# A second place for transposed exponentials, a planner that counts transfers at a shared rate, and ten pairs with native scores

## The chip, the core and the metric

One core of a Trainium2 chip runs the whole computation. The metric is the device time of one execution in microseconds. Five engines work side by side, each on its own instruction stream in program order: TensorE (PE in the profile, with its weight loads as PEld), VectorE (DVE), ScalarE (ACT), GpSimd (POOL) and SyncE (SP). Here SyncE does nothing but start DMA transfers, one after the other, and it too waits at the head of its queue.

## What is computed

The reference computes attention with a block-causal mask (blocks of 64) for 8 batches of 8 heads, 576 positions, head size 64, and then a bilinear feed-forward of its result (4608 tokens, width 512, inner width 1536).

```python
scores = scale * np.matmul(q, k.transpose(0, 1, 3, 2))
scores = np.where(block_i >= block_j, scores, -1000000000.0)
attn = np.exp(scores - np.max(scores, axis=-1, keepdims=True))
attn = attn / (np.sum(attn, axis=-1, keepdims=True) + 1e-09)
x = np.matmul(attn, v)            # heads side by side
out = (x @ w_a) * (x @ w_b) @ w_out
```

The feed-forward weights come as 64-bit floats, read as pairs of 32-bit words: the kernel itself converts them to two 32-bit parts ("hi" and "lo").

## The kernel before

The work falls in two. First comes attention, two heads at a time ("pair" p, 32 of them, four to a batch), with a first feed-forward pass over the first third of the inner width (`F1 = 4` blocks of 128) woven between. Then come two more passes over the rest of the width (from line 1077 on), which TensorE fills alone. Names carry batch and head: `x1_6` belongs to batch 1, heads 6 and 7, which is pair 7.

Most products are made from "split" operands: a value is a high part plus a low part, and three products (hi hi, hi lo, lo hi) make one. Scores of the first `NATIVE` pairs are instead made by one plain 32-bit product that the program writes as one matmul and the profile shows as two; such a pair needs a scaling of q on GpSimd (L448). Other pairs need four steps: `qh` and `kh` on ScalarE (L454, L462), `ql` on VectorE (L458), `kl` on GpSimd (L466).

A pair goes through these steps:

- SyncE loads q and k (`take`, L397) and v (L402).
- TensorE makes scores in two rounds, because there are only two score banks in PSUM, `x` and `y`: first `C3` and `C1`, then, when the exponentials have freed the banks, `C2` and `C0` (L482).
- VectorE masks and takes negated maxima (L501, L509 to L518); ScalarE makes exponentials with their sums (L528); VectorE adds and inverts the sums (`rc`, L557 to L562); GpSimd normalizes in ten steps (L571).
- The exponentials have to be transposed. For pairs 0 to 3 TensorE does it and ScalarE copies the result into the tile `at` (L593, L599). From pair 4 on VectorE transposes blocks of 32 by 32 into a tile `bl` (L576, L581; there are two, for even and odd pairs), and SyncE starts 16 copies per pair that carry the blocks to their partitions in `at` (`move`, L621). There is one `at`: a pair's copies wait for the value product of the pair before.
- TensorE makes the value product (60 matmuls, L630). ScalarE evacuates it into `xf` (L648, L649), SyncE stores it (L663), and ScalarE and GpSimd split it (L669, L673).

The first pass of the feed-forward, once a batch's four pairs are through, consists of groups of 12 matmuls (L234): per half batch eight groups for the two inner products, whose product is split again (`hf` on VectorE L722, `hh` on ScalarE, `hl` on GpSimd), and four groups for the output (`pso`). They have the lowest priority on TensorE and run strictly in order; this text calls them fillers.

At the start twelve weight conversions (steps `cd`, `cs`, `cr`, `cm`, `cf`, `cg`, `cx`, `ch`, `cl`, L863 to L876) run beside the first pairs, six of the steps on VectorE and ScalarE between the attention's. They use a raw tile with two buffers (`fetch`, L136) and three scratch tiles `s`, `m`, `x`. A second lot of conversions for the later passes starts after the last pair's scores (`start_conv2`).

The order of everything up to the last pair is set by a planner (`plan`, L342). It holds a table `TOOK` (engine time, time until others see the result) for each kind of step, plays the steps through, and always takes the ready step with the lowest key on the engine that is free first; the result is written down engine by engine, and the chip follows that order. `SLOTS` gives the keys of a pair's steps relative to others, `CONV_STEP` the keys and earliest times of the conversions. It is a plan only: on the chip an instruction starts when the real semaphores allow it.

```python
last_v = [got("V", p - 1)]
...
ds = ... [Op("D", SP_, lambda i=i, g=g: move(i, g), [o for o in (got("T", p), got("V", p - 1)) if o], ...
```

Of the kernel before, what the change touches and what calls it, by code (L numbers as in the profile page):

```python
# [9 lines left out]
F32 = mybir.dt.float32  # L10
F32R = mybir.dt.float32r
I32 = mybir.dt.int32
# [8 lines left out]
EPS = 1e-9  # L21
WARM = 9

NATIVE = 6
MM = 3
MORE = 8 - MM
XB = 3
PET = 4
A_KEY = 18
SLOTS = [12.0] * 6 + [14.6] * 26  # L30
CONV_STEP = 6.5
CONV_KEY = 12.0
CONV_LO = True
KEEP_UNTIL, KEEP_EVERY = 66.0, 2.5
SWITCH = 0.1
LAGS = {"PE": 0.24, "DVE": 0.14, "Activation": 0.17, "Pool": 0.1, "SP": 2.0}
TOOK = {
# [12 lines left out]
    "posta": (0.29, 0.17, 0), "postb": (0.375, 0.14, 0), "posto": (0.29, 0.17, 0), "hh": (0.338, 0.16, 0),  # L50
# [16 lines left out]
def attention_then_bilinear_ffn(  # L67
# [65 lines left out]
            tc.add_manual_dep(ins.ins, last[key].ins.name, NOSYNC, reason="after work that is waited for")  # L133


    def fetch(src, nm):  # L136
        raw = wpool.tile([P, 512, 2], I32, tag="raw", name=f"raw{nm}", bufs=2)
        nc.sync.dma_start(raw.rearrange("p n w -> p (n w)"), src)
        return raw

    def convert(raw, nm, paced, own=False):

        hi, mid = raw[:, :, 1], raw.bitcast(U16)[:, :, 1]
        s, m, x = (wpool.tile([P, 512], I32, tag=f"cv_{x}", name=f"{x}{nm}") for x in "smx")
        sf, mf, xf = (t.bitcast(F32) for t in (s, m, x))
        v = nc.vector

        def step(ins):
            if paced:
                behind_of(ins, "hf")  # L150


        step(v.tensor_scalar(s, hi, 20, 0x7FF, op0=ALU.logical_shift_right, op1=ALU.bitwise_and))
        nc.scalar.activation(s, s, AF.Relu, scale=2.0 ** 23, bias=shift)
        yield

        step(v.tensor_scalar(m, hi, 0xFFFFF, 0x100000, op0=ALU.bitwise_and, op1=ALU.bitwise_or))
        yield
        step(v.scalar_tensor_tensor(mf, mid, 2.0 ** -16, m, op0=ALU.mult, op1=ALU.add))
        yield  # L160
        step(v.scalar_tensor_tensor(s, hi, -0x80000000, s, op0=ALU.bitwise_and, op1=ALU.bitwise_or))
        yield
        step(v.tensor_tensor(xf, mf, sf, op=ALU.mult))
        if own:
            yield
        return xf, mf
# [71 lines left out]
    hpool = pool(ctx, "hpool", 1)  # L238

    def h_tile(kind, n, dt, nm):  # L240
        return hpool.tile([P, T2], dt, tag=f"h{kind}", name=nm, bufs=(10, 6)[kind])[:, :n]

    def ab_unit(f, xs, n, nm, hs):

# [97 lines left out]
    def plan():  # L342
        free = dict.fromkeys(LAGS, 0.0)
        ready = {e: [] for e in LAGS}
        users = [[] for _ in ops]
        left = [len(o.deps) for o in ops]
        for o in ops:
            for d, plus in o.deps:
                users[d.n].append((o, plus))
            if not o.deps:  # L350
                ready[o.eng].append(o)
        out = []
        mode = 0
        held = []

        def since(o):
            if not o.frees:
                return o.at
            if len(held) < MM:
                return o.at  # L360
            r = held[-MM]
            return o.at if r is o else 1e9 if r.end is None else max(o.at, r.end)

        while any(ready.values()):
            t, e = min((max(free[e], min(map(since, q))), e) for e, q in ready.items() if q)
            o = min((o for o in ready[e] if since(o) <= t), key=lambda o: (o.key, o.n))
            if o.frees:
                held.append(o.frees)
            ready[e].remove(o)
            free[e] = t + o.took + (SWITCH if e == PE_ and o.mode != mode else 0)  # L370
            if e == PE_:
                mode = o.mode
            if o.also:
                free[ACT_] = max(free[ACT_], t) + o.also
            o.start, o.end = t, free[e] + o.lag
            out.append(o)
            for u, plus in users[o.n]:
                u.at = max(u.at, o.end + plus)
                left[u.n] -= 1
                if not left[u.n]:  # L380
                    ready[u.eng].append(u)
        assert len(out) == len(ops)
        return out
# [37 lines left out]
    def got(what, p):  # L421
        return done.get((what, p))

    def attention(p):
# [158 lines left out]

        def new_at():
            if "at" not in st:
                st["at"] = apool.tile([P, NQ, 2, NE_, QB], F32, tag="at", name=f"at{n}", bufs=1)
            return st["at"]

        def pe_turn(t, h):
# [10 lines left out]
                           st["tp", t, h][:, :m * P].rearrange("p (c g q) -> p c g q", g=NQ, q=QB))  # L600

        by_pe = p < PET
        last_v = [got("V", p - 1)]
        prev = got("rc", p)
        for i, t in enumerate((LAST, 2, 1, 0, NT)):
            for h in range(2):
                prev = add("N", POOL_, lambda t=t, h=h: norm(t, h), [prev, got("rc", p)], 13 + i, kind=f"N{t}")
                if by_pe:
                    o = add("T", PE_, lambda t=t, h=h: pe_turn(t, h), [prev], 14 + i, kind=f"P{t}")
                    o.frees = add("A", ACT_, lambda t=t, h=h: place(t, h), [o, *last_v], A_KEY + i, kind=f"A{t}")  # L610
                    ts.append(o.frees)
                elif t != NT:
                    ts.append(add("T", DVE_, lambda t=t, h=h: turn(t, h),
                                  [prev, ("D", p - 2)], 17 + i, kind=f"T{t}"))
# [4 lines left out]
        def move(i, g):  # L619
            new_at()  # L620
            nc.sync.dma_start(st["at"][QB * g:QB * (g + 1), i], bl[QB * i:QB * (i + 1), g])  # L621

        ds = ts if by_pe else [Op("D", SP_, lambda i=i, g=g: move(i, g), [o for o in (got("T", p), got("V", p - 1)) if o],
                 key=B0 + 23) for i in range(NQ) for g in range(NQ)]
        done["D", p] = Op("none", SP_, lambda: None, ds, key=B0 + 16 if by_pe else B0 + 23)

# [21 lines left out]
            nc.scalar.copy(st["xf"][:, :BLK], st["av0"][:, :BLK])  # L648
            nc.scalar.copy(st["xf"][:, BLK:], st["av"])  # L649

        vs = [("D", p), ("lv", p), ("X", p - 1)]
        for c in range(NCH):
            o = add("V", PE_, lambda c=c: values(c), vs, 18 if by_pe else 27, mode=2, kind=f"V{c}")
            done[f"V{c}", p] = o
# [177 lines left out]
    def conversion(k, f, i):  # L832
# [13 lines left out]
            st["raw"] = fetch(wab[f, :, i] if i < KP else wo[f], nm)  # L846

        def tile_of(x):
            if x not in st:
                st[x] = wpool.tile([P, 512], I32, tag=f"cv_{x}", name=f"{x}{nm}")  # L850
            return st[x]

        def hi_w():
# [48 lines left out]
        raw = fetch(wab[F1, :, 0], f"w{F1}_0")  # L902
        box["g"] = convert_w(parts(range(F1, F1 + F2)), nc.vector, paced=True, raw=raw)

    o = Op("st", SP_, start_conv2, [done["C0", NP - 1]], key=base[-1] + 10)
    for k in range(EARLY):
        o = Op("cv1", DVE_, lambda: next(box["g"]), [o, done["rc", NP - 1]], key=base[-1] + 20 + k)
    with tc.manual_schedule(engines={getattr(mybir.EngineType, e) for e in LAGS}):
# [269 lines left out]
```

## Time and profile before

| | us |
|---|---|
| three runs | 1192.08, 1196.36, 1200.49 |
| median | 1196.36 |
| the profiled execution | 1189.79 |
| its span, first to last instruction | 1188.0 |
| its mean granted TensorE clock | 0.983 |

A row of a timeline gives the start, the length, the engine, the line, the operation with its output and inputs, the number of instructions merged, and in brackets the idle time before it and what ended it. A row of a stretch gives busy microseconds (and instructions) for PE, PEld, DVE, ACT and POOL, then the granted clock as a share of full speed, the DMA engines' busy share and GB/s. A row of waits reads "who <- whom: total us, times, longest". Matmuls overlap, so the time that one adds is read from start to start.

### The profile page before, as it was taken

The page shows a single profiled execution, that of the slowest core. Times are in us where ns is not written, and L with a number is a line of the kernel's source. Part 1 is how long each engine was busy: PE and PEld are TensorE (multiplying, and loading weights), DVE is VectorE, ACT ScalarE, POOL GpSimd, SP SyncE. Part 2 cuts the span into 40 slices and gives each one's busy share as a digit, 9 for nine tenths or more (in the row PEclk, how much of TensorE's full clock was granted, in tenths as well). Part 3 has the DMA queues.
Part 4 walks back from the last instruction along what each step waited for, and adds up shares of the span by engine and source line. Part 5 has one row for each costly group of instructions (what it writes and reads, how often), then busy time and mean ns, then how long its engine had stood idle before and what let it go on. Part 6 is the DMA issues. An engine that isn't in the chain of part 4 may idle for free.

```text
span 1188.0 us, 23207 instructions
## 1 busy us (share of the span) xinstructions
PE 1113.1 (94%) x8440; PEld 1051.2 (88%) x8440; DVE 869.0 (73%) x1817; ACT 546.5 (46%) x1430; POOL 377.6 (32%) x553
## 2 busy tenths in 40 slices
PE   5878879999999998989799999999999999999998
PEld 3557768888988898989799999999999999999998
DVE  5789787767767776764499897787887867767754
ACT  4886556665656655553364443433433312222210
POOL 4777666564656565553000201201202000000000
PEclk7999889999999999999899999999999999999999
DMA  4444767777677777767634635626679325235031
GB/s 156 156 158 131 194 172 200 198 199 208 191 193 203 199 207 197 196 183 210 177 113 130 164 101 149 166 67 157 165 254 290 91 71 160 54 106 160 1 107 67
DMA packets 85553, 187.13 MB, mean 158 GB/s; under 512 B 14272, under 2 KB 40896, under 8 KB 85440
## 3 DMA queue, kind: packets, MB, share of 16 engines
q1 hardware_dynamic: 78528, 176.21, 50.6%
q0 software_dynamic: 6912, 9.44, 5.0%
q8 instruction: 67, 1.10, 0.4%
q14 instruction: 46, 0.38, 0.1%
HBM read 87.03 MB, written 47.19 MB: 113 GB/s over the span
## 4 chain that ended last, share of the span: by engine, by line
PE 49%; issue 11%; DVE 9%; DMA 8%; SPq 6%; ACT 6%; POOL 4%; DVEq 0%; ACTq 0%; POOLq 0%
PE pso_z L1029 14%; PE psx_z L983 8%; PE psw_z L983 8%; PE psv_z L983 8%; SPq L621 5%; DMA qr<-qT 4%; PE psy_z L983 4%; ACT e L528 3%; PE ps L234 3%; POOL e L571 3%; PE av L630 3%; DVE nm L501 2%; DMA at<-bl 2%; DVE bl L576 2%; PE x L482 1%
## 5 line engine op out<-in xcount | busy, mean ns | idle before, releaser
L234 PE MATMUL ps<-xh,wab 128*128 128x288 f32 x1024 | 212.6, 298 | 0.0
L1029 PE MATMUL pso_z<-h_z,wo 128*128 128x384 f32 x1152 | 203.3, 334 | 0.0
L1029 PEld LDWEIGHTS pso_z<-h_z,wo 128*128 128x128 f32 x1152 | 199.9, 188 | 0.4 <-ACT h_z L124 0.3
L234 PEld LDWEIGHTS ps<-xh,wab 128*128 128x128 f32 x1024 | 166.3, 189 | 4.6 <-issue 3.4
L571 POOL TENSOR_SCALAR e<-e,rc 128x512 f32<-128x512 f32 (+3 forms) x256 | 155.1, 623 | 34.3 <-DVE rc L562 34.2
L234 PE MATMUL ps<-xl,wab 128*128 128x288 f32 x512 | 153.6, 300 | 1.5 <-POOL xl L673 1.3
L576 DVE STREAM_TRANSPOSE bl<-e 128x512 f32<-128x512 f32 (+1 forms) x224 | 116.2, 579 | 48.7 <-DMA at<-bl 31.3
L1093 POOL DMA_DIRECT2D part<-pt x48 | 43.0, 1056 | 298.9 <-ACT pt L1092 293.7
L124 ACT CAST h_z<-u_z 128x384 fp32r<-128x384 f32 x96 | 49.4, 515 | 175.7 <-DVE u_z L1008 160.0
L630 PE MATMUL av<-at,v 128*64 128x128 f32 (+1 forms) x1920 | 104.9, 265 | 23.1 <-DMA at<-bl 18.6
L630 PEld LDWEIGHTS av<-at,v 128*64 128x64 f32 x1920 | 98.4, 142 | 31.5 <-issue 19.3
L983 PE MATMUL psx_z<-xh,wab 128*128 128x384 f32 x384 | 116.0, 338 | 2.3 <-DVE u_z L1001 2.3
L983 PE MATMUL psv_z<-xh,wab 128*128 128x384 f32 x384 | 116.2, 337 | 0.0
L983 PE MATMUL psw_z<-xh,wab 128*128 128x384 f32 x384 | 116.1, 338 | 0.0
L234 PE MATMUL pso<-hh,wo 128*128 128x288 f32 x480 | 101.6, 300 | 0.0
L234 PEld LDWEIGHTS ps<-xl,wab 128*128 128x128 f32 x512 | 96.6, 189 | 5.1 <-issue 2.3
L482 PE MATMUL x<-k,q 64*128 64x512 f32 (+1 forms) x360 | 63.8, 457 | 32.4 <-ACT e L528 24.8
L234 PEld LDWEIGHTS pso<-hh,wo 128*128 128x128 f32 x480 | 78.4, 189 | 3.3 <-issue 2.2
L528 ACT ACTIVATE e<-y,nm 128x192 f32<-128x192 f32 (+1 forms) x128 | 61.7, 486 | 28.2 <-DVE nm L501 26.0
L501 DVE TENSOR_REDUCE nm<-x 128x2 f32<-128x1024 f32 x64 | 72.9, 1140 | 2.4 <-PE x L482 1.7
L983 PEld LDWEIGHTS psx_z<-xh,wab 128*128 128x128 f32 x384 | 71.0, 187 | 2.8 <-DVE u_z L1001 2.6
L730 POOL TENSOR_TENSOR hl<-hf,hh 128x288 fp32r<-128x288 f32 x56 | 45.8, 818 | 84.2 <-ACT hh L726 81.8
(135 smaller groups left out, 2325.8 us busy)
## 6 DMA issues: line engine op xcount, KB each, us to landing
at<-bl SPq DMA_DIRECT2D x448, 112.0 KB, 2.3
xr<-xd SPq DMA_DIRECT2D x48, 384.0 KB, 4.1
raww<-wab SPq DMA_DIRECT2D x24, 512.0 KB, 4.3
v<-vm SPq DMA_DIRECT2D x32, 320.0 KB, 3.3
xd<-xf SPq DMA_DIRECT2D x32, 288.0 KB, 2.5
part<-ob SPq DMA_DIRECT2D x64, 144.0 KB, 2.7
part<-pt POOLq DMA_DIRECT2D x48, 192.0 KB, 7.2
pt<-part SPq DMA_DIRECT2D x48, 192.0 KB, 3.2
```

Of the source, the lines that this page charges most:

```text
L124: nc.scalar.copy(hi, src)
L234: nc.tensor.matmul(ps, w_, d_, start=(i == 0), stop=(i == n - 1))
L482: nc.tensor.matmul(out[:, h], qq[r, q0[t]:q0[t] + P], keys, start=j == 0, stop=j == len(qk) - 1)
L501: nc.vector.tensor_reduce(st["nm"][:, :, t], view, axis=AX.X, op=ALU.max, negate=True)
L528: nc.scalar.activation(out, view, AF.Exp, bias=bias, accum_out=sm[:, h, t, :1])
L571: nc.gpsimd.tensor_scalar(ev, ev, st["rc"][:, h, t:t + 1], 1.0, op0=ALU.mult, op1=ALU.mult)
L576: nc.vector.transpose(dst, es[h][t].rearrange("p (c g q) -> p c g q", g=NQ, q=QB))
L621: nc.sync.dma_start(st["at"][QB * g:QB * (g + 1), i], bl[QB * i:QB * (i + 1), g])
L630: nc.tensor.matmul(out[d], v[:, h, c], a[:, qs, h, e_], start=start, stop=stop, skip_group_check=True)
L730: nc.gpsimd.tensor_tensor(lo, box2["hf"], f32(hi), op=ALU.subtract)
L983: nc.tensor.matmul(ps, wt[:, i, iw], j[:, ix], start=start and kp == 0 and i == 0 and j is xh, stop=kp == KP - 1 and i == 1, skip_group_ch ...
L1029: nc.tensor.matmul(ps, wt[:, a, osl], b, start=i == 0, stop=i == 3 * len(fs) - 1)
```

## The change

It has three parts.

1. The conversions' raw and scratch tiles become views of one tile of 14336 bytes per partition (`BIG`, `cv_views`), and `at` is of the same size. From pair 7 on, when the first twelve conversions are through, odd pairs up to 29 take that space for their `at`; even pairs, and pairs 30 and 31, keep the old one. So a pair's copies depend on the value product two pairs back instead of one; pair 7's depend on the conversions, and the second lot of conversions starts after value product 29.
2. The planner knows transfers' sizes (`KB`) and lets them land one after the other at a shared rate (`RATE`), corrects some times in `TOOK`, adds 0.3 us to whatever TensorE takes from another engine (`SLACK`), and has other keys (`SLOTS`, `CONV_STEP`). A value product is planned after the splits and the store of the result two pairs back. All this only moves instructions.
3. `NATIVE` goes from 6 to 10: pairs 6 to 9 drop their four split steps.

```diff
-NATIVE = 6
+NATIVE = 10
+AT2 = 7
+BIG = 3584
+KB = {"lk": 288, "lq": 320, "lv": 320, "cd": 512, "D": 112, "st": 144, "xd": 288}
+RATE, LATENCY = 250.0, 1.9
+SLACK = 0.3
-SLOTS = [12.0] * 6 + [14.6] * 26
-CONV_STEP = 6.5
+SLOTS = [12.0] * 12 + [15.2] * 20
+CONV_STEP = 7.5
...
-    "D": (0.6, 1.7, 0), ...
+    "D": (0.64, 1.75, 0), ...
...
+    def cv_views():
+        if box_big[0] is None:
+            t = new_big("cv").bitcast(I32)
+            box_big[0] = {
+                "raw": [t[:, 1024 * i:1024 * (i + 1)].rearrange("p (n w) -> p n w", w=2) for i in range(2)],
+                **{x: t[:, 2048 + 512 * i:2560 + 512 * i] for i, x in enumerate("smx")}}
+        return box_big[0]
...
             o.start, o.end = t, free[e] + o.lag
+            if o.kind in KB:
+                bus = max(bus, t + LATENCY - 0.3) + KB[o.kind] / RATE
+                o.end = bus + 0.3
             out.append(o)
             for u, plus in users[o.n]:
-                u.at = max(u.at, o.end + plus)
+                u.at = max(u.at, o.end + plus + (SLACK if u.eng == PE_ and e != PE_ else 0))
...
             if "at" not in st:
-                st["at"] = apool.tile([P, NQ, 2, NE_, QB], F32, tag="at", name=f"at{n}", bufs=1)
+                if AT2 <= p < NP - 2 and p % 2:
+                    box_big[0] = None
+                    st["at"] = new_big(f"at{n}").rearrange("p (i h e q) -> p i h e q", i=NQ, h=2, e=NE_)
+                else:
+                    st["at"] = apool.tile([P, NQ, 2, NE_, QB], F32, tag="at", name=f"at{n}", bufs=1)
...
-        last_v = [got("V", p - 1)]
+        at_free = [got("V", p - (2 if AT2 < p < NP - 1 else 1)), got("V", p - 2)] if p != AT2 or p % 2 == 0 else [x["cl"] for x in conv_ops]
...
-        vs = [("D", p), ("lv", p), ("X", p - 1)]
+        vs = [("D", p), ("lv", p), ("X", p - 1), ("S1", p - 2), ("xd", p - 2)]
...
-    o = Op("st", SP_, start_conv2, [done["C0", NP - 1]], key=base[-1] + 10)
+    o = Op("st", SP_, start_conv2, [done["C0", NP - 1], done["V", NP - 3]], key=base[-1] + 10)
```

More of the change, by code (lines that the diff above doesn't have):

```diff
@@ L27 @@
 XB = 3
+AT2 = 7
+BIG = 3584
+HB = 10, 6
+KB = {"lk": 288, "lq": 320, "lv": 320, "cd": 512, "D": 112, "st": 144, "xd": 288}
+RATE, LATENCY = 250.0, 1.9
+SLACK = 0.3
 PET = 4
 A_KEY = 18
-SLOTS = [12.0] * 6 + [14.6] * 26
-CONV_STEP = 6.5
+SLOTS = [12.0] * 12 + [15.2] * 20
+CONV_STEP = 7.5
 CONV_KEY = 12.0
@@ L133, in behind_of, with new_big @@
             tc.add_manual_dep(ins.ins, last[key].ins.name, NOSYNC, reason="after work that is waited for")
+    box_big, box_n = [None], [0]
+    def new_big(nm):
+        return wpool.tile([P, BIG], F32, tag="big", name=nm)
+    def cv_views():
[5 more added lines that the diff above has]
+        return box_big[0]
     def fetch(src, nm):
-        raw = wpool.tile([P, 512, 2], I32, tag="raw", name=f"raw{nm}", bufs=2)
+        raw = cv_views()["raw"][box_n[0] % 2]
+        box_n[0] += 1
         nc.sync.dma_start(raw.rearrange("p n w -> p (n w)"), src)
@@ L143, in convert @@
         hi, mid = raw[:, :, 1], raw.bitcast(U16)[:, :, 1]
-        s, m, x = (wpool.tile([P, 512], I32, tag=f"cv_{x}", name=f"{x}{nm}") for x in "smx")
+        s, m, x = (cv_views()[x] for x in "smx")
         sf, mf, xf = (t.bitcast(F32) for t in (s, m, x))
@@ L240, in h_tile @@
     def h_tile(kind, n, dt, nm):
-        return hpool.tile([P, T2], dt, tag=f"h{kind}", name=nm, bufs=(10, 6)[kind])[:, :n]
+        return hpool.tile([P, T2], dt, tag=f"h{kind}", name=nm, bufs=HB[kind])[:, :n]
     def ab_unit(f, xs, n, nm, hs):
@@ L353, in plan @@
         mode = 0
+        bus = 0.0
         held = []
@@ L602, in attention @@
         by_pe = p < PET
-        last_v = [got("V", p - 1)]
+        at_free = [got("V", p - (2 if AT2 < p < NP - 1 else 1)), got("V", p - 2)] if p != AT2 or p % 2 == 0 else [x["cl"] for x in conv_ops]
+        if p == AT2 + 1 - AT2 % 2 and p > AT2:
+            at_free += [x["cl"] for x in conv_ops]
         prev = got("rc", p)
@@ L609, in attention @@
                     o = add("T", PE_, lambda t=t, h=h: pe_turn(t, h), [prev], 14 + i, kind=f"P{t}")
-                    o.frees = add("A", ACT_, lambda t=t, h=h: place(t, h), [o, *last_v], A_KEY + i, kind=f"A{t}")
+                    o.frees = add("A", ACT_, lambda t=t, h=h: place(t, h), [o, *at_free], A_KEY + i, kind=f"A{t}")
                     ts.append(o.frees)
@@ L621, in move @@
             nc.sync.dma_start(st["at"][QB * g:QB * (g + 1), i], bl[QB * i:QB * (i + 1), g])
-        ds = ts if by_pe else [Op("D", SP_, lambda i=i, g=g: move(i, g), [o for o in (got("T", p), got("V", p - 1)) if o],
+        ds = ts if by_pe else [Op("D", SP_, lambda i=i, g=g: move(i, g), [o for o in (got("T", p), *at_free) if o],
                  key=B0 + 23) for i in range(NQ) for g in range(NQ)]
@@ L848, in tile_of @@
         def tile_of(x):
-            if x not in st:
-                st[x] = wpool.tile([P, 512], I32, tag=f"cv_{x}", name=f"{x}{nm}")
+            st[x] = cv_views()[x]
             return st[x]
```

10 rows, old and new, of the table TOOK are left out of this document.

## The prediction

> **What bounds the kernel now.** I read the page first, then the busy times by stage, what TensorE waits for, its timeline at those waits, and last SyncE's timeline, because it starts the transfers that one of those waits ends on. Pairs are numbered 0 to 31 (pair 7 is `1_6` in the names: batch 1, head 6). "Filler" is a matmul of the first feed-forward pass (L234): every batch of four pairs brings 288 of them, 72 per pair.
>
> ```profile
> span 1188.0 us, 23207 instructions
> PE 1113.1 (94%) x8440; PEld 1051.2 (88%) x8440; DVE 869.0 (73%) x1817; ACT 546.5 (46%) x1430; POOL 377.6 (32%) x553
> ...
> 60.00:90.00 30.00, 23.25 (x220) 16.14 (x220) 24.68 (x46) 24.07 (x74) 23.81 (x28) 1.00 0.51 165
> 90.00:120.00 30.00, 25.11 (x227) 21.44 (x225) 29.21 (x66) 19.62 (x61) 21.11 (x30) 1.00 0.49 128
> ...
> 420.00:450.00 30.00, 28.22 (x298) 25.78 (x297) 21.70 (x50) 18.06 (x58) 16.10 (x25) 1.00 0.74 204
> 600.00:630.00 30.00, 30.00 (x218) 29.79 (x216) 29.13 (x65) 19.40 (x40) 0.00 (x0) 1.00 0.53 153
> ```
>
> The columns are TensorE, its weight loads, VectorE, ScalarE, GpSimd, the granted clock and the DMA share. There are four stages. To about 88 us no engine is full: a chain through all of them sets the pace. From 90 to 120 VectorE is full (29.21 of 30). From 200 to 560 TensorE leads with 28.2 of 30. After about 580 TensorE has no gap to speak of, and the change leaves that stage's instructions alone: about 606 us stay. The question is what TensorE loses before 580.
>
> ```profile
> PE x L482 <- ACT e L528: 24.8, 19, 6.5
> PE av L630 <- DMA at<-bl: 18.6, 12, 4.7
> ...
> 123.97 1.49 PE L482 MATMUL x<-k,q 64*128 64x448 f32 x6 [6.52 <-ACT e L528]
> 158.37 1.30 PE L482 MATMUL x<-k,q 64*128 64x448 f32 x6 [4.09 <-ACT e L528]
> 162.82 5.39 PE L630 MATMUL av<-at,v 128*64 128x128 f32 x56 [2.14 <-DMA at<-bl]
> 293.45 0.96 PE L482 MATMUL x<-k,q 64*128 64x512 f32 x6 [1.32 <-ACT e L528]
> 404.42 2.87 PE L630 MATMUL av<-at,v 128*64 128x128 f32 x56 [0.29 <-PE av L630]
> 540.88 2.87 PE L630 MATMUL av<-at,v 128*64 128x128 f32 x56 [0.74 <-DMA at<-bl]
> 559.08 1.11 PE L630 MATMUL av<-at,v 128*64 128x128 f32 x17 [1.17 <-DMA at<-bl]
> 569.36 0.34 PE L630 MATMUL av<-at,v 128*64 128x64 f32 x4 [2.43 <-DMA at<-bl]
> 574.44 4.79 PE L630 MATMUL av<-at,v 128*64 128x128 f32 x56 [4.74 <-DMA at<-bl]
> ```
>
> Two waits carry the loss: second score products waiting for the exponentials that free their bank, and value products waiting for the transposed exponentials to land. Long waits cost twice: 56 value matmuls take 2.87 us normally, 5.39 and 4.79 us after the gaps.
>
> ```profile
> 124.00:128.00 4.00, 4.00 (x18) 3.14 (x20) 3.98 (x9) 1.76 (x7) 3.36 (x8) 0.51 0.80 215
> 160.00:164.00 4.00, 1.86 (x20) 1.53 (x20) 1.86 (x5) 2.15 (x8) 0.00 (x0) 0.50 0.85 240
> 296.00:300.00 4.00, 4.00 (x22) 4.00 (x23) 2.60 (x9) 0.45 (x2) 2.72 (x5) 0.68 0.57 132
> ```
>
> The clock fell to about 0.5 after the gaps of 6.52 and 4.09 us and to 0.68 after one of 1.32. Work done slowly cost about 2 us at 124, 4 at 160 (5.39 for 2.87, and the scores around it), 1.3 at 296 (0.32 x 4) and 1.9 at 574: 9 us. The Trainium skill ("TensorE: Matmul & The Clock Gate", section "What's actually happening") says that the clock halves after an idle window of about 3.4 us; the rows at 160 and 574 agree, the one at 296 does not, and by the rule the loss would be about 8 instead of 9.
>
> ```profile
> 236.49 1.78 SPq L621 DMA_DIRECT2D at<-bl  x3
> 238.31 0.59 SPq L663 DMA_DIRECT2D xd<-xf  x1
> 238.94 9.24 SPq L621 DMA_DIRECT2D at<-bl  x13
> 252.83 2.65 SPq L621 DMA_DIRECT2D at<-bl  x3
> ...
> DMA to landing us min/median/max: 2.1/2.3/4.9
> ...
> SPq L621 <- PE av L630: 65.7, 25, 5.7
> DVE bl L576 <- DMA at<-bl: 31.3, 13, 4.2
> ```
>
> This is the loop that sets the middle stage. The one `at` buffer is free when a value product ends; only then do the 16 copies of the next pair start (SyncE waited 65.7 us for that); they last 11.7 us (236.49 to 248.18) and land 2.3 later; then the next value product runs, 2.9. That is 16.9 us, and the copies do restart after 16.3 (252.83). The value products of eight pairs between 404.42 and 540.88 are 17.06 us apart.
>
> **The change, part by part.**
>
> *Startup (pairs 0 to 5).* The planner's new costs, key steps and its 7.5 us per conversion move conversion steps on VectorE. At pair 3's first maximum, on VectorE before:
>
> ```order
> L562 RECIPROCAL rc0_4_458<-rc0_4_458 128x10
> L872 TENSOR_TENSOR xw2_1_616<-mw2_1_528,sw2_1_525 128x512
> L863 TENSOR_SCALAR sw3_0_629<-raww3_0_537 128x512
> L866 TENSOR_SCALAR mw3_0_631<-raww3_0_537 128x512
> L868 SCALAR_TENSOR_TENSOR mw3_0_631<-raww3_0_537,mw3_0_631 128x512
> L501 TENSOR_REDUCE nm0_6_647<-x0_6_0_620 128x2
> ```
>
> And after the change (`cv` is the tile that now holds all of a conversion):
>
> ```order
> L586 RECIPROCAL rc0_4_433<-rc0_4_433 128x10
> L899 SCALAR_TENSOR_TENSOR cv_161<-cv_161 128x512
> L901 TENSOR_TENSOR cv_161<-cv_161 128x512
> L525 TENSOR_REDUCE nm0_6_611<-x0_6_0_594 128x2
> L533 MEMSET y0_6_1_605 64x2x64
> ```
>
> The next conversion's three opening steps no longer stand ahead of the maximum; they come after the biases.
>
> ```profile
> 68.96 1.13 PE L482 MATMUL x<-k,q 64*128 64x512 f32 x4
> 69.52 0.81 DVE L863 TENSOR_SCALAR sw<-raww 128x512 int32<-128x512 int32 x1
> 71.60 1.21 DVE L501 TENSOR_REDUCE nm<-x 128x2 f32<-128x1024 f32 x1
> ...
> 65.88 3.15 PE L630 MATMUL av<-at,v 128*64 128x64 f32 x60 [0.52 <-ACT at L599]
> 81.50 3.15 PE L630 MATMUL av<-at,v 128*64 128x64 f32 x60 [1.07 <-ACT at L599]
> ```
>
> The maximum's bank was full at 70.1 (68.96 + 1.13) and it began at 71.60: 1.5 us may go. A pair takes 15.6 us here (65.88 to 81.50), and two things alternate in it: scores to sums, which gets shorter, and normalizing, turning and the value product, which doesn't (GpSimd is at 23.81 of 30). So I count half to two thirds of 1.5, 1.0 us for each of five pairs, and 1 for pair 0, whose maximum stands behind one conversion step instead of four: **-6**; ends 0 (the other half decides) and -10 (all of it).
>
> *Native pairs 6 to 9.* Each loses its split steps (`q` on VectorE, others on ScalarE and GpSimd) and pays in TensorE time.
>
> ```profile
> L458 DVE SCALAR_TENSOR_TENSOR q<-qr,q 128x640 fp32r<-128x640 f32 x26 | 28.2, 1086 | 6.1 <-ACT q L454 5.6
> ...
> 70.78 1.09 PE L593 MATMUL tp<-ident,e 128*128 128x128 f32 x8
> ...
> 99.49 0.96 PE L482 MATMUL x<-k,q 64*128 64x512 f32 x6
> 101.15 0.40 PE L234 MATMUL ps<-xh,wab 128*128 128x288 f32 x1
> ```
>
> The first two score products take 1.82 us native (68.96 to 70.78) and 1.66 split (99.49 to 101.15); twice that for the other two gives 0.32 a pair, **+1.3** for four (ends 0 and +3). VectorE drops 4 x 1.09 us, most of it where it is full or where a late `q` held it up before the gap at 158.
>
> *88 to 200 us.* The waits named above sum to 12.8 (6.52, 4.09, 2.14) and 6 of slow clock. Pair 7's second product follows its first with only four fillers between in both orders, so that wait stays; two `q` steps of 1.09 us leave a VectorE that is full there, and I take 2 off the 6.52 and leave its slow clock. Before pair 9's second product there now stand 32 fillers and a value product (32 x 0.138 + 2.9, rows below) in place of 20 fillers, and no `q` step: 4 off. The 2.14 and the slow clock behind it go with the buffer: 6 off. Another 1 for small ones: **-13**; ends -4 and -18.
>
> *The second buffer, pairs 8 to 30.* Copies of pair p now wait for value product p-2. SyncE's queue at pair 10, before and after:
>
> ```order
> L402 DMA v2_4_2487<-vm 128x640
> L397 DMA kr3_2_2490<-kT 128x576
> L397 DMA qr3_2_2512<-qT 128x640
> L621 DMA at2_4_2576<-bl0_133 32x896 x3
> L663 DMA xd_57<-xf2_2_2584 128x576
> L621 DMA at2_4_2576<-bl0_133 32x896 x13
> ```
>
> ```order
> L426 DMA v2_4_2272<-vm 128x640
> L651 DMA at2_4_2310<-bl0_133 32x896 x6
> L693 DMA xd_57<-xf2_2_2351 128x576
> L651 DMA at2_4_2310<-bl0_133 32x896 x10
> L421 DMA kr3_2_2491<-kT 128x576
> L421 DMA qr3_2_2497<-qT 128x640
> ```
>
> The copies no longer start on the heels of value product 9 (whose result `xf2_2` stands among them): six go before its result is out. They moved ahead of the loads of pair 13, whose scores run two pairs later. The value product itself moved about half a pair earlier on TensorE. With the loop open, TensorE's own work sets the pace:
>
> ```profile
> 306.65 5.51 PE ps L234 x40
> 283.08 3.00 PE L630 MATMUL av<-at,v 128*64 128x64 f32 x60
> 107.44 0.88 PE L482 MATMUL x<-k,q 64*128 64x448 f32 x6 [0.23 <-ACT e L528]
> 108.98 0.58 PE L482 MATMUL y<-k,q 64*128 64x192 f32 x6
> ```
>
> 72 fillers at 0.138 are 9.9, a value product 2.9, split scores 1.66 + 0.8 + 0.5: 15.8 us against 17.06, so 1.2 a pair for about 20 pairs (200 to 541) is the most there is: -24. The least is 0. The scores' waits for exponentials stay on the same engines, and only the planner's 0.3 us of slack works on them, so I take a little over half: **-14**. Late next will be those scores.
>
> *Tail (pairs 30, 31).* These two share a buffer as before. ScalarE shows what stands between their two evacuations, one row per filler group, before and after:
>
> ```order
> L649 COPY xf7_4_7893<-av7_4_7854 128x512
> L669 CAST xh7_4_0_7903<-xf7_4_7893 128x288
> L726 CAST hh_6_1_2_7925<-hf_6_1_2_7918 128x288
> L718 COPY a_6_1_3_7939<-ps0_6_1_3_7912 128x288
> L669 CAST xh7_4_1_7952<-xf7_4_7893 128x288
> L726 CAST hh_6_1_3_7959<-hf_6_1_3_7955 128x288
> L648 COPY xf7_6_8002<-av07_6_7971 128x64
> ```
>
> ```order
> L679 COPY xf7_4_7531<-av7_4_7484 128x512
> L748 COPY a_6_0_2_7546<-ps0_6_0_2_7477 128x288
> L174 ACTIVATE cv_7463<-cv_7463,shift_67 128x512
> L756 CAST hh_6_0_2_7571<-hf_6_0_2_7564 128x288
> L748 COPY a_6_0_3_7585<-ps0_6_0_3_7559 128x288
> L699 CAST xh7_4_0_7603<-xf7_4_7531 128x288
> L756 CAST hh_6_0_3_7614<-hf_6_0_3_7606 128x288
> L748 COPY a_6_1_0_7628<-ps0_6_1_0_7598 128x288
> L756 CAST hh_6_1_0_7653<-hf_6_1_0_7646 128x288
> L784 COPY ob12_0_7667<-pso_12_0_7641 128x288
> L784 COPY ob12_1_7683<-pso_12_1_7662 128x288
> L678 COPY xf7_6_7726<-av07_6_7691 128x64
> ```
>
> On TensorE 36 fillers became 100: 13.8 us of cover for copies that need 11.7 + 2.3. Waits of 1.17, 2.43 and 4.74 and 1.9 of slow clock can go, 10.2: **-8**; ends -3 and -10. Behind pair 31, 88 fillers (12 us) now cover what the next stage waits for.
>
> *Costed at nothing:* the box for the conversions (the same waits, instruction by instruction), the value product's new planned dependences (its evacuation waited for the same before), the second conversion's start behind value product 29 (whose result leaves SyncE's queue before it). For waits that I don't see I add **+3** (0 to +10).
>
> **Sum.** -6 +1.3 -13 -14 -8 +3 = -36.7 against the profiled execution's own 1189.79 us (span 1188.0): 1153. That execution was 6.6 us under the median of the three runs (1196.36), so on the median I forecast **1160 us**.
>
> **Rivals.** *The buffer frees nothing* (likely if the turned blocks themselves are late: VectorE's 31.3 us of waits for landed copies speak against it): the middle's -14 and the startup's -6 fall away, 1180. *Nor does the early stretch gain* (VectorE full at 29.21 there speaks for it): pair 7 to 9 give -4 instead of -13, 1189: no change to speak of. *Slower:* every value product now comes half a pair sooner, and copies take 14.0 us of a 15.8 us pair, so a turned block that is 1.8 us late shows on TensorE one to one. A wait of 1.7 us on each of 22 pairs (36.7 / 22) uses up the gain; at the 2.43 us of the row at 569.36, 22 x 2.43 = 53 makes 1213. The Trainium skill ("DMA: Bandwidth & Descriptors", section "Issuing engines are not separate DMA queues") says that all transfers interleave on the same 16 DMA engines, which speaks against starting copies earlier among loads. The longest landing, 4.9 instead of 2.3, would do it alone. Against it: the DMA share is 0.74 now and the bytes stay.
>
> **Chances.** My forecast 0.74, with its own range 1138 to 1178; the buffer frees nothing 0.10; no gain early either 0.09; slower 0.07. A measurement of this kernel can tell about 1%, 12 us. Faster by more than that (under 1184): 0.74 + 0.10 = 0.84; within it 0.09; slower 0.07. The range goes from 1138 (the terms' far ends: -10 +0 -18 -20 -10 = -58, the middle not quite at its end) to 1186, which leaves out the slower case, most of the unchanged one and a few hundredths below.
>
> **What would show it.** Startup: value products under 15 us apart, first filler at 80 to 84. Pairs 7 to 9: one wait of 4 us or so with a slow clock instead of three. Middle: SyncE's wait for value products nearly gone, VectorE's for landed copies too, pairs 16.2 to 16.5 us apart. Tail: no wait over 1 us before the last value products. I am wrong if value products wait longer in total than 18.6 us, if VectorE stays full past 128 us, or if the stage after 580 takes more than 606 us.

## The result and the profile after

| | us |
|---|---|
| before, four runs: median (lowest to highest) | 1194.22 (1190.63 to 1200.49) |
| after, four runs: median (lowest to highest) | 1162.62 (1160.34 to 1162.96) |
| ratio of the runs, 95% interval | 0.9726 (0.968 to 0.9772) |
| profiled execution after, its span | 1162.46, 1160.5 |

The change makes the kernel 2.3 to 3.2% faster; 1160 was forecast. Medians, ratios and single times in the experiments below are those of undisturbed runs. Between the profiled executions the span fell by 27.5 us. The first question is where. Busy times by stretch of the kernel before, cut at the first filler, about 4.5 us after pair 12's first score product, some 25 us after pair 31's, and at the first product of the second phase (columns as in the prediction: TensorE first):

```profile
0.00:86.40 86.40, 64.01 (x501) 40.93 (x501) 62.23 (x128) 61.24 (x180) 55.17 (x86) 0.92 0.47 152
86.40:200.00 113.60, 95.16 (x888) 83.89 (x888) 94.32 (x207) 65.40 (x207) 73.54 (x106) 0.92 0.65 176
200.00:541.00 341.00, 323.28 (x3241) 298.71 (x3238) 235.67 (x557) 201.42 (x639) 197.72 (x306) 0.99 0.73 197
541.00:624.10 83.10, 74.66 (x652) 73.66 (x652) 53.99 (x123) 35.97 (x78) 8.15 (x9) 0.96 0.57 166
624.10:1188.00 563.90, 555.99 (x3170) 553.99 (x3168) 422.80 (x807) 182.51 (x328) 42.96 (x48) 1.00 0.46 129
```

And after the change, cut at the corresponding places:

```profile
0.00:82.10 82.10, 64.43 (x500) 41.43 (x500) 62.53 (x127) 59.03 (x176) 52.37 (x86) 0.94 0.49 156
82.10:192.00 109.90, 97.02 (x900) 82.07 (x899) 88.01 (x207) 63.34 (x208) 68.16 (x107) 0.97 0.73 199
192.00:517.00 325.00, 318.60 (x3200) 290.16 (x3200) 241.53 (x561) 200.26 (x636) 198.59 (x306) 0.99 0.77 209
517.00:598.50 81.50, 78.14 (x640) 77.69 (x637) 50.92 (x114) 35.02 (x77) 7.46 (x9) 0.96 0.48 140
598.50:1160.50 562.00, 555.96 (x3170) 554.05 (x3168) 422.69 (x807) 182.25 (x328) 42.88 (x48) 1.00 0.46 130
```

Length minus TensorE's busy time is what TensorE idled: 22.4, 18.4, 17.7, 8.4 and 7.9 us before, 17.7, 12.9, 6.4, 3.4 and 6.0 after. So 4.7 us of waiting went at startup, 5.6 in the early stretch, 11.3 in the middle, 5.1 in the tail and 1.9 in the second phase, 28.6 in all, while TensorE's busy time grew by 1.0 (1113.1 to 1114.2). The cuts do not stand at the same instruction of TensorE's order, since value products and fillers moved across them, so it is the idle time of a stretch, and not its length, that can be set side by side.

What TensorE still waits for, after the change:

```profile
PE x L506 <- ACT e L552: 17.5, 12, 5.4
PE av L660 <- DMA at<-bl: 6.4, 3, 5.1
PE av L660 <- DMA part<-ob: 3.4, 1, 3.4
```

The waits for landed copies fell from 18.6 us to 6.4, those for exponentials from 24.8 to 17.5. (The row that names `part<-ob` is pair 31's value product; it reads no tile of that store, so the last of its copies is the likelier cause.) TensorE's long waits, and the clock behind them:

```profile
115.99 1.86 PE L506 MATMUL x<-k,q 64*128 64x448 f32 x4 [4.26 <-ACT e L552]
154.00 4.29 PE L660 MATMUL av<-at,v 128*64 128x128 f32 x56 [5.13 <-DMA at<-bl]
536.72 5.39 PE L660 MATMUL av<-at,v 128*64 128x128 f32 x56 [3.36 <-DMA part<-ob]
...
116.00:120.00 4.00, 4.00 (x14) 2.21 (x15) 3.76 (x9) 1.30 (x6) 3.39 (x7) 0.57 0.80 186
154.00:158.00 4.00, 4.00 (x53) 4.00 (x54) 3.89 (x6) 1.51 (x3) 3.03 (x5) 0.63 1.04 303
```

The first is the one that the prediction kept at pair 7 (6.52 us before). The second and third were not foreseen. The pace of the middle is read from the first score products of pairs 12 and 31, after the change and then before:

```profile
187.61 0.96 PE L506 MATMUL x<-k,q 64*128 64x512 f32 x6
491.95 1.36 PE L506 MATMUL x<-k,q 64*128 64x512 f32 x6 [1.28 <-ACT q L478]
```

```profile
195.50 0.96 PE L482 MATMUL x<-k,q 64*128 64x512 f32 x6
516.68 0.96 PE L482 MATMUL x<-k,q 64*128 64x512 f32 x6 [1.08 <-ACT e L528]
```

That is 304.3 us for 19 pairs, 16.02 each, where it was 16.90. Not all of it is gained: the stretch between these two rows holds 18 value products instead of 19 and 1325 fillers instead of 1349, some 6 us of work that runs elsewhere. What is gained is idle time of TensorE, which fell in this stretch from 17.2 to 5.6 us. Value products wait 0.3 us in it where they waited 9.0, and score products wait for exponentials 1.2 us (bank `x`) where it was 6.7.

**Where the two unforeseen waits come from.** SyncE's queue before pair 7's value product, after the change:

```profile
128.47 1.15 SPq L651 DMA_DIRECT2D at<-bl  x2
...
132.00 8.15 SPq L651 DMA_DIRECT2D at<-bl  x13
140.19 0.58 SPq L426 DMA_DIRECT2D v<-vm  x1
140.87 6.82 SPq L651 DMA_DIRECT2D at<-bl  x10
147.79 0.53 SPq L693 DMA_DIRECT2D xd<-xf  x1
148.36 3.68 SPq L651 DMA_DIRECT2D at<-bl  x6
```

The copies started from 128.47 to 140.15 are pair 6's, the next sixteen pair 7's. Pair 7 is the first with the second buffer, so its copies wait for no value product; they wait for SyncE, which starts them one by one behind pair 6's. Pair 6's could start only when value product 5 had ended, at 128.4. TensorE had nothing else to run: the order has 8 fillers between the last scores and value product 7, and the next filler in their strict order belongs to the second batch and needs pair 7's own result. In the tail it is a weight load that stands ahead of pair 31's copies, on SyncE and then VectorE:

```profile
515.64 0.39 SPq L158 DMA_DIRECT2D cv<-wab  x1
516.08 0.44 SPq L426 DMA_DIRECT2D v<-vm  x1
516.57 6.60 SPq L158 DMA_DIRECT2D cv<-wab  x2
523.35 0.51 SPq L651 DMA_DIRECT2D at<-bl  x1
...
520.73 0.43 DVE L173 TENSOR_SCALAR cv<-cv 128x512 int32<-128x512 int32 x1 [4.63 <-DMA cv<-wab]
522.13 0.68 DVE L181 SCALAR_TENSOR_TENSOR cv<-cv 128x512 int32<-128x512 int32 x1
```

The third load of a second-phase weight goes into the half of the raw space that the first filled, so it waits until VectorE has read that (522.13 + 0.68 = 522.81) and starts at 522.85. Value product 30 had ended, and freed the buffer, at 519.6 (516.76 + 2.87); pair 31's copies started at 523.35.

### The profile page after: what moved, and what is told of

Read it like the earlier page. It is cut to its first block, busy times and chain, and to the rows that moved or that the text cites. A ratio compares the mean times of both kernels' runs of the same rounds, so it can differ in the third digit from the quotient of the medians.

```text
span 1160.5 us, 23135 instructions
## 1 busy us (share of the span) xinstructions
PE 1114.2 (96%) x8400; PEld 1045.4 (90%) x8400; DVE 865.7 (75%) x1813; ACT 539.9 (47%) x1422; POOL 369.5 (32%) x553
## 4 chain that ended last, share of the span: by engine, by line
PE 74%; DVE 7%; ACT 6%; DMA 5%; SPq 3%; POOL 3%; issue 2%; ACTq 0%; DVEq 0%; POOLq 0%
PE pso_z L1058 16%; PE ps L254 10%; PE psx_z L1012 9%; PE psw_z L1012 9%; PE psv_z L1012 9%; PE pso L254 6%; PE av L660 5%; PE psy_z L1012 4%; PE x L506 3%; ACT e L552 3%; SPq L651 3%; DVE nm L525 2%; PE y L506 2%; DMA qr<-qT 1%; POOL e L595 1%
## 5 line engine op out<-in xcount | busy, mean ns | idle before, releaser
L595 POOL TENSOR_SCALAR e<-e,rc 128x512 f32<-128x512 f32 (+3 forms) x256 | 150.6, 607 | 45.3 <-DVE rc L586 45.3
L600 DVE STREAM_TRANSPOSE bl<-e 128x512 f32<-128x512 f32 (+1 forms) x224 | 119.5, 583 | 14.8 <-POOL e L595 10.2
L660 PE MATMUL av<-at,v 128*64 128x128 f32 (+1 forms) x1920 | 101.3, 264 | 10.4 <-DMA at<-bl 6.4
L506 PE MATMUL x<-k,q 64*128 64x512 f32 (+1 forms) x344 | 66.1, 479 | 23.5 <-ACT e L552 17.5
```

Source lines behind the costliest of these rows:

```text
L506: nc.tensor.matmul(out[:, h], qq[r, q0[t]:q0[t] + P], keys, start=j == 0, stop=j == len(qk) - 1)
L595: nc.gpsimd.tensor_scalar(ev, ev, st["rc"][:, h, t:t + 1], 1.0, op0=ALU.mult, op1=ALU.mult)
L600: nc.vector.transpose(dst, es[h][t].rearrange("p (c g q) -> p c g q", g=NQ, q=QB))
L660: nc.tensor.matmul(out[d], v[:, h, c], a[:, qs, h, e_], start=start, stop=stop, skip_group_check=True)
```

## The experiments

All ran beside the kernel before, on the same chip. Ratios are to it, and its own median moved by up to 3.6 us between these sessions (1191.17 to 1194.78). "Planner's numbers" are `TOOK`, `KB` with `RATE` and `LATENCY` (the shared rate), `SLACK`, `SLOTS` and `CONV_STEP`.

| kernel | median, us | ratio to before (95% interval) |
|---|---|---|
| after | 1162.62 | 0.9726 (0.968 to 0.9772) |
| no_buffer | 1201.62 | 1.0059 (1.0025 to 1.0094) |
| old_planner | 1187.30 | 0.9965 (0.9938 to 0.9991) |
| buffer_alone | 1193.02 | 1.0004 (0.9973 to 1.0036) |
| native6 | 1163.26 | 0.9763 (0.9725 to 0.98) |
| slack0 | 1156.90 | 0.9692 (0.9638 to 0.9747) |
| costs_old | 1184.20 | 0.9904 (0.9866 to 0.9942) |
| steps_old | 1161.48 | 0.9732 (0.9694 to 0.9771) |
| tail | 1157.06 | 0.969 (0.9646 to 0.9734) |
| no_rate | 1164.06 | 0.9748 (0.97 to 0.9797) |
| buf_costs | 1173.03 | 0.9824 (0.9777 to 0.9871) |
| slack0_tail | 1153.47 | 0.9654 (0.9583 to 0.9725) |
| sp_dur | 1166.09 | 0.9787 (0.9757 to 0.9817) |

**Is it the buffer or the planner?** Four kernels.

`no_buffer`:

```diff
-AT2 = 7
+AT2 = 99
```

> The changed kernel with one buffer for the transposed exponentials throughout (conversions still in the shared tile; new planner and ten native pairs kept). Theory A, the prediction's: the second buffer alone opens the loop of value product, 16 copies, value product. Then the middle stage falls back from 16.0 to about 17 us a pair, the value products wait for landed copies some 18 us again, SyncE waits about 60 us for value products, and the time is 1178 to 1186 (before: 1194, after: 1163). Rival B: the planner's order, with transfers at a shared rate, does most of it, and the copies are hidden with one buffer too: 1163 to 1170, pairs under 16.5 us apart.

`old_planner`, and `buffer_alone`, which has `NATIVE = 6` besides:

```diff
-KB = {"lk": 288, "lq": 320, "lv": 320, "cd": 512, "D": 112, "st": 144, "xd": 288}
+KB = {}
-SLACK = 0.3
+SLACK = 0.0
-SLOTS = [12.0] * 12 + [15.2] * 20
-CONV_STEP = 7.5
+SLOTS = [12.0] * 6 + [14.6] * 26
+CONV_STEP = 6.5
-    "lk": (0.44, 3.5, 0), "lq": (0.43, 3.5, 0), "lv": (0.5, 4, 0), ...
+    "lk": (0.33, 3.5, 0), "lq": (0.33, 3.5, 0), "lv": (0.33, 4, 0), ...
```

> The changed kernel with the planner's numbers of before (no shared rate, no slack, old costs, key steps and 6.5 us a conversion); second buffer and ten native pairs kept. Theory A: only the startup's 4 to 6 us and a part of the waits for exponentials come back, since the buffer needs no planner: 1168 to 1175, first filler at about 86 us, pairs in the middle about 16.3 us apart. Rival B: the buffer is worth little unless the planner places copies and value products earlier: 1182 or more, with waits for landed copies near 18 us. Rival C: the planner's numbers do nothing by themselves: 1163 to 1166.

> The kernel before with the second buffer alone (old planner's numbers, six native pairs). Theory A: the middle stage gains most of its 17 us and the wait behind pair 9 goes, so 1172 to 1180; SyncE's 65.7 us of waiting for value products falls to under 20. Rival B: without the planner the copies are placed no earlier and the gain is under 6 us: 1188 to 1194.

`native6`: `NATIVE = 6`, all else as after.

> The changed kernel with six native pairs instead of ten. Theory A: the native pairs cost 1.3 us of TensorE and save 2 to 6 us of waits where VectorE is full (90 to 130 us), so that without them it is 1163 to 1168. Rival B: the relief of VectorE is what lets pairs 6 to 9 run and without it the waits of 6.5 and 4 us return with their slow clock: 1170 to 1176. Rival C: they only cost: 1160 to 1162.

Measured: without the buffer the planner's numbers make the kernel 0.3 to 0.9% slower than before; without the numbers the buffer gains 0.1 to 0.6%, or nothing with six native pairs. Neither is worth more than a few us by itself, together they take 32 us. The native pairs are worth nothing that can be told. Theory A, that the buffer is enough, has fallen; the rival "worth little unless the planner places the work" stands, though not in its own detail (it looked for 18 us of waits for copies). `no_buffer` was slower than either theory had it. A good part is one place, the value product of pair 31 in its two parts (that of pair 30 ran at 566.16 without a wait):

```profile
580.37 0.48 PE L660 MATMUL av<-at,v 128*64 128x64 f32 x4 [9.86 <-DMA at<-bl]
584.23 5.39 PE L660 MATMUL av<-at,v 128*64 128x128 f32 x56 [3.38 <-DMA at<-bl]
```

The rest of `no_buffer` is the middle: 17.28 us a pair between the first score products of pairs 12 and 31, with 19 value products and 1344 fillers as before, and 17.5 us of idling. Its value products hardly wait there (1.1 us); its score products do, 14.6 us, for exponentials and for split q. SyncE waits 85.0 us for value products, more than the 65.7 of before.

`buffer_alone` shows the other half. Its waits, which can be set beside those of before (24.8 and 18.6):

```profile
PE x L506 <- ACT e L552: 26.5, 18, 6.6
...
PE av L660 <- DMA at<-bl: 7.4, 5, 2.1
```

The loop did open: 11.2 us of waits for copies went, and SyncE waits 2.7 us for value products. Pair 28's first score product came 13.3 us earlier than before, and yet the second phase began 2.1 us later; the two rows of `buffer_alone`, then of before:

```profile
452.11 0.73 PE L506 MATMUL x<-k,q 64*128 64x512 f32 x4
626.18 0.34 PE L1012 MATMUL psy_z<-xh,wab 128*128 128x384 f32 x1
```

```profile
465.45 0.96 PE L482 MATMUL x<-k,q 64*128 64x512 f32 x6 [0.40 <-ACT e L528]
624.11 0.34 PE L983 MATMUL psy_z<-xh,wab 128*128 128x384 f32 x1
```

The order explains it: `buffer_alone` leaves 656 fillers for the time behind the last scores, where before left 564. These 92 fillers at 0.1325 us are 12.2 us. The scores were moved ahead of fillers, and the fillers came later; TensorE's waits for exponentials stayed. In all TensorE idled 68.5 us, 6.4 less than before, but its busy time is 7.1 us longer (1120.2 against 1113.1) for the same instructions. What lengthened them is not shown. A marker that comes earlier is no gain while work that it was moved past is still to be done.

**Which of the planner's numbers?** `slack0` (`SLACK = 0.0`), `costs_old` (`KB = {}` and the old `TOOK`) and `steps_old` (the old `SLOTS` and `CONV_STEP`), each undone alone, all else as after.

> The changed kernel without the planner's 0.3 us of slack for TensorE. The first runs showed that neither the buffer nor the planner's numbers gain anything alone (1193 and 1187 without the planner's numbers, 1202 without the buffer, each against 1194), so the question is which of the numbers the buffer needs. Theory A: the slack, since it leaves more fillers between the second and the third score product (44 to 52 with it, 40 without), so that TensorE doesn't wait for exponentials: without it 1171 or more, waits for exponentials over 25 us. Rival B: the costs of transfers, and the slack is worth under 4 us: 1163 to 1167.

> The changed kernel with the old costs of the planner (no shared rate of transfers, old durations of loads, copies and the second score product), but with its slack, key steps and conversion steps. The order leaves 648 fillers for the time behind the last score product, as with all numbers old (656), where the changed kernel leaves 608: 40 fillers of 0.1325 us, 5 us, that run alone at the end instead of covering waits. Theory A (slack): 1163 to 1168. Rival B (costs): 1175 to 1187, near the 1187 with all numbers old.

> The changed kernel with the old key steps (12.0 for six pairs, then 14.6) and 6.5 us a conversion, but with its new costs and slack. Theory A and rival B both: only the startup's 4.3 us come back, first filler at about 86 us: 1165 to 1169. Rival C: the steps carry the gain: 1175 or more.

It is the costs, as rival B said: 1184. The slack gains nothing; without it the median is 5.7 us lower, and its times (1155.95 to 1157.43) lie below all four of after, though the intervals of the two ratios overlap. The steps make no difference in the end, where 1165 to 1169 was expected. They do at first: in `steps_old` the first filler went back from 82.13 to 87.99, and pair 12's first score product from 187.61 to 193.10, with 352 fillers between the two in either kernel. It is made up later, most visibly at value product 31, which waits 1.40 us instead of 3.36 and keeps the full clock (2.87 us instead of 5.39 for 56 products). What the old costs do is seen on ScalarE ahead of five first score products in the middle of `costs_old`. One of them, ScalarE's rows and then TensorE's:

```profile
412.70 0.67 ACT L486 CAST k<-kr 128x576 fp32r<-128x576 f32 x1 [3.64 <-DMA kr<-kT]
413.28 0.39 ACT L748 COPY a<-ps 128x288 f32<-128x288 f32 x1
414.76 0.74 ACT L478 ACTIVATE q<-qr 128x640 fp32r<-128x640 f32 x1 [1.09 <-DMA qr<-qT]
415.40 0.62 ACT L552 ACTIVATE e<-x,nm 128x448 f32<-128x448 f32 x1
...
416.01 0.62 ACT L552 ACTIVATE e<-x,nm 128x448 f32<-128x448 f32 x1
...
416.78 0.97 PE L506 MATMUL x<-k,q 64*128 64x512 f32 x6 [3.46 <-ACT e L552]
```

Two exponentials that free the bank stand in ScalarE's queue behind the split steps of a later pair's k and q, and those wait 3.64 and 1.09 us for loads that haven't landed. TensorE waits 3.46. At 235.49, 299.82, 332.05 and 503.61 it is the same picture, with waits of 2.87, 2.09, 2.83 and 1.44 on TensorE and a q split that waited 2.15, 1.79, 1.80 and 0.62 directly ahead of the exponentials. The five waits on TensorE sum to 12.7 us, as much as the middle lost: between the first score products of pairs 12 and 31 TensorE idled 18.2 us in `costs_old` and 5.6 in after. The planner presumably had put the splits there because in its play the loads had long landed; no run shows its play.

**Which costs?** `no_rate` is the changed kernel with `KB = {}` alone; `sp_dur` is that with TensorE's own durations old too, so that of all new costs only those of SyncE's issues are left:

```diff
-    "C1": (0.78, 0.24, 0), ... "mm4": (0.528, 0.24, 0),
+    "C1": (0.623, 0.24, 0), ... "mm4": (0.5225, 0.24, 0),
```

> The changed kernel without the planner's shared rate of transfers alone (each transfer again ends a fixed time after its issue), all other numbers new. With rate and durations both old it took 1184, so one of the two carries 20 us or both do. Theory A: the rate, because only it makes the planner see that 16 copies and the loads share one path: 1178 to 1186, with 28 us of waits for exponentials as there. Rival B: the durations, above all that of the second score product (0.78 for 0.62 us), after which the first product of the next pair is placed: 1160 to 1166, and waits for exponentials near 17 us.

> The changed kernel without the shared rate (which made no difference) and with the old durations of TensorE's own work (0.62 us for the second score product, 0.5225 for four fillers), so that of the new costs only the durations on SyncE's queue stay: loads 0.43 to 0.50 for 0.33 us, copies 0.64 for 0.60, stores 0.50 for 0.33. Theory A: SyncE's durations carry it, since the order on TensorE then again sets a value product between nearly every two pairs: 1160 to 1168. Rival B: TensorE's durations are needed, since without them the planner sets the next pair's first product too early: 1176 to 1186, as with all costs old (1184).

The shared rate, which gave the change its name, does nothing that can be told. The durations on SyncE's queue carry most of it: 1166, against 1164 with TensorE's durations new too and 1184 with all costs old (by the ratios 14 us of 21). In the middle TensorE idles 5.8 us in `sp_dur`, as in after, and its waits for exponentials there fell from 13.9 us in `costs_old` to 4.5. Which of these durations does it, those of loads, copies or stores, no run tells apart. ScalarE's waits for landing k and q loads between 150 and 600 us, first of `costs_old`, then of `sp_dur`:

```profile
ACT k L486 <- DMA kr<-kT: 23.1, 12, 3.6
ACT q L478 <- DMA qr<-qT: 14.2, 14, 2.1
```

```profile
ACT k L486 <- DMA kr<-kT: 12.9, 10, 4.2
ACT q L478 <- DMA qr<-qT: 11.2, 15, 1.8
```

37.3 us became 24.1; `buffer_alone` has 42.3 by the same two rows, after 26.0. The new numbers are close to the trace: the rows above have loads of v at 0.58 and 0.44 us of SyncE's time (old table 0.33, new 0.50). The Trainium skill ("DMA: Bandwidth & Descriptors", section "Issuing engines are not separate DMA queues") calls the time to initiate a DMA usually small relative to the DMA itself. For one copy the trace agrees: a start takes some 0.6 us (13 in 8.15) and the copy lands in 2.3. For the sixteen of a pair it does not: SyncE starts them in 11.7 us (128.47 to 140.15, with three other starts between), so that the starts are the larger part, and a planner that had SyncE's starts too short lost some 18 us (1184.2 against 1166.1).

**Are buffer and costs enough?** `buf_costs`: after with `SLACK`, `SLOTS`, `CONV_STEP` and `NATIVE` as before.

> The kernel before with the second buffer and the new costs (durations and shared rate) alone: six native pairs, old key steps and conversion steps, no slack. Theory: these two together are what gains, so 1155 to 1166. Rival: the other numbers (steps, slack, native pairs) have a share that shows only when all are missing: 1170 or more.

1173: the two carry two thirds of the gain. The rest is lost before pair 12: its first score product stands at 198.16, 10.5 us later than in after, and the granted clock between the first filler and there is 0.89 where after has 0.97. (The middle, to 496.21, seems faster than after with 15.69 us a pair, but it holds 68 fillers less, 9 us that are paid behind it; TensorE idles 7.3 us in it against 5.6.) Undoing the steps alone (`steps_old`) puts pair 12 5.5 us later and undoing the native pairs alone (`native6`) 2.0, and `slack0`, where pair 12 comes at 186.83, speaks against the slack. So the loss at pair 12 looks like roughly the sum of the two (12 fillers more, 1.6 us, stand before it as well). Why `steps_old` and `native6` make theirs up by the end and `buf_costs` does not is not shown.

**The tail, and a faster version.** `tail` keeps the order of after but for one load:

```diff
-            nc.sync.dma_start(st["at"][QB * g:QB * (g + 1), i], bl[QB * i:QB * (i + 1), g])
+            last["D" if p == NP - 1 else "-"] = nc.sync.dma_start(st["at"][QB * g:QB * (g + 1), i], ...)
...
-        nc.sync.dma_start(raw.rearrange("p n w -> p (n w)"), src)
+        behind_of(nc.sync.dma_start(raw.rearrange("p n w -> p (n w)"), src), "D")
```

> The changed kernel with one order changed on SyncE: the third load of a second-phase weight (which waits until VectorE has read the first out of the shared tile) goes behind the copies of pair 31 instead of ahead of them. Theory A: that load holds the copies up (they start at 523.4, 3.8 us after value product 30 ended at 519.6), so that the 3.36 us of TensorE's wait for the value product of pair 31 and the slow clock behind it (5.39 us for 56 products instead of 2.87) go: 1157 to 1160 against 1162.6. Rival B: the 16 copies take 9 us for themselves and TensorE runs out of fillers anyway: 1161 to 1164.

`slack0_tail` has this and `SLACK = 0.0`.

> The changed kernel without slack and with the third weight load of the second phase behind the copies of pair 31. Theory: the two gains (1157.2 and 1157.1 against 1162.6) are at different places, but without slack the value product of pair 31 waited 2.6 us and no slow clock followed, so the second is worth 2.6 there: 1154 to 1156. Rival: the order without slack has its own wait there, and nothing is added: 1156 to 1158.

In `tail` pair 31's copies start at 523.91, right behind value product 30 (521.02 + 2.87), and the value product:

```profile
538.25 2.87 PE L660 MATMUL av<-at,v 128*64 128x128 f32 x56 [0.68 <-DMA part<-ob]
```

It waits 0.68 us instead of 3.36 and runs at full clock, 5.2 us in all; the medians differ by 5.6. How much of this reaches the kernel's time is less sure: the intervals of the two ratios overlap widely, and the profiled executions differ by 1.7 us (1160.80 against 1162.46). In that of `tail` pair 31's first score product came 3.7 us later (495.64 against 491.95) in an order that is the same until there, so that single executions differ by as much. Both changes together give 1153.5, the fastest version found, 9.1 us under after by the medians; the intervals of the two ratios overlap a little, the single times (1152.31 to 1155.29 against 1160.34 to 1162.96) don't.

## Why the prediction was right, and where it wasn't

The time was right to 2.6 us, partly by luck; its steps were less so.

- *The sum.* 36.7 us were predicted against the profiled execution of before, 27.3 came (1189.79 to 1162.46). That 1160 was hit owes something to the next step: I added 6.6 us because the profiled execution of before lay so far under its median. After the change the two agree (1162.46 and 1162.62). The error of 9 in the sum and this one nearly cancel, and that is luck.
- *Startup, -6.* The first filler came at 82.13, inside the 80 to 84 named, and 4.7 us of waiting went. The value products there are 14.2 to 14.9 us apart, under the 15 named. As far as pair 12 the term holds: in `steps_old` the startup's gain is gone and pair 12 comes 5.5 us later. That the time of `steps_old` is the same all the same shows that this term doesn't simply add to the others: a different order behind it met shorter waits.
- *Native pairs, +1.3.* Not to be told from zero, inside its ends.
- *88 to 200 us, -13.* By idle time -5.6; the term counted the slow clock too, and the stretch's granted clock rose from 0.92 to 0.97, so the gain is larger than that, by how much isn't worked out. The wait at pair 7's second score product kept 4.26 of 6.52 us, with a slow clock, and the one at pair 9's went, as written. The step that failed is that "the 2.14 and the slow clock behind it go with the buffer": this wait, value product 7's, grew to 5.13 and kept its slow clock. One buffer still served pair 6, and SyncE's queue is serial.
- *The second buffer, -14.* In the middle 11.3 us of idling went, near the size predicted (the pace of 16.02 us a pair, under the 16.2 to 16.5 named, says more than was gained, since work left the stretch). The loop was read rightly: 8.7 us of it are waits of value products, and without the buffer the middle idles 17.5 us again, though in other waits (`no_buffer`). What was missed is the condition. "The scores' waits for exponentials stay on the same engines, and only the planner's 0.3 us of slack works on them" was wrong: the slack was no help, and with the buffer but the old costs (`costs_old`) waits for exponentials took 13.9 us of the middle, against 1.2 after the change. The durations of SyncE's starts, which the prediction did not price at all, decided the order on ScalarE and with it the waits (4.5 us in `sp_dur`). SyncE's copies now wait 6.3 us for value products instead of 65.7, and VectorE's turns 1.9 us for landed copies instead of 31.3, as named; but such waits went in `buffer_alone` as well, without a gain in time.
- *Tail, -8.* 5.1 us of idling went, but the last value product kept a wait of 3.36 us and its slow clock. "No wait over 1 us before the last value products" was missed. I had costed the second conversion's start at nothing, looking only at its first load; its third load stood ahead of the copies and waited for VectorE. In `tail`, where it stands behind them, the wait is 0.68 us.
- *The rivals.* "The buffer frees nothing" (1180) did not come. The buffer alone did gain nothing (1193), but for another reason than that rival gave: the turned blocks were not late, VectorE waited 3.5 us for landed copies there. The slower case did not come either; value products waited 9.8 us in total, not 37.

Left open: whether pair 5 or 6 in the second buffer would take away the wait at value product 7 (not tried); what the value product's two new planned dependences and the conversions' shared tile do, since every run above but the kernel before has them; and why the changed kernel's times spread over 3 us where those of the kernel before spread over 7 to 16 (and those of `tail` over 8).

## What to carry to other kernels

A buffer that opens a loop gains nothing until the order uses it: look whether the engine's waits fell, not whether a stage's marker moved, and count the work that was pushed behind it. In a planned order the cheap-looking costs of the queue that starts transfers matter as much as those of the engines, because a step planned behind a load that lands late holds up everything in its engine's queue. When two resources share a tile, follow each later user of it, not only the first, on every queue that it stands in.

## What was unexpected of the hardware

How far TensorE's clock fell did not follow from the length of the wait before it. In `buffer_alone` 56 value matmuls took 4.52 us after a wait of 2.07 (granted clock 0.66 from 544 to 549), in `slack0` 2.87 after 2.60 (1.00 from 532 to 535):

```profile
544.30 4.52 PE L660 MATMUL av<-at,v 128*64 128x128 f32 x56 [2.07 <-DMA at<-bl]
```

```profile
532.20 2.87 PE L660 MATMUL av<-at,v 128*64 128x128 f32 x56 [2.60 <-DMA part<-ob]
```

In the changed kernel waits of 0.99 us before 328.86 and 0.35 before 330.56 were followed by a clock of 0.59 from 332 to 335. The Trainium skill ("TensorE: Matmul & The Clock Gate", section "What's actually happening") has the clock halve after at least one idle window of about 3.4 us, a window that runs freely. The rows of 0.99 and 2.07 us do not agree with that as it reads, since each wait is shorter than the window. That a wait's place in the window counts could set 2.07 apart from 2.60, but no run here tested it.
